# Selective attention and a SwiGLU block on one core: every transpose on TensorE, no DRAM scratch, loads in another order

## The chip, the cores and the metric

The kernel runs on one core of one Trainium2 chip. The metric is device time in microseconds (us) of one launch, the median of several runs. A profiled execution has a time of its own, and inside it the span that the trace covers.

## What is computed

Inputs are q, k and v of 8 batches x 8 heads x 576 positions x 64, a gate s of 8 x 8 x 576, and the three matrices of a gated feed-forward block (FFN): 512 x 1536 twice, and 1536 x 512. All are float32; the output is 4608 x 512 float32.

```python
scores = scale * q @ k^T                       # per batch and head, causal
cum  = cumsum(maximum(s, 0))                   # along the positions
bias = -(cum[i] - cum[j])
attn = softmax(where(causal, -1e9, scores + minimum(bias, 0)))
x    = (attn @ v), heads side by side          # 4608 x 512
g    = x @ w_gate
out  = (g * sigmoid(g) * (x @ w_val)) @ w_out
```

## The kernel before

**Attention.** The 64 heads (batch x head) are numbered in one row, `bh`, and grouped in 16 blocks `hb` of four. A block's q and k are loaded as float32 with positions on partitions (`load_qk`, L105), cast to bf16 in pairs of heads (`cast_one`, L170), and have to be turned so that the 64 features lie on partitions. Two heads share one turned tile. The bias goes into the same matmul: the partitions that the pair's other head would take hold rows with the cumulative sum as a high and a low bf16 part, and rows of ones (`aug`, L155, copies such rows for one block; they were written once to a DRAM tensor `augd` at L153). So one matmul per piece gives score plus bias. Each head's causal half is cut into four score pieces of at most 512 columns (`score_piece`, L253). ScalarE takes their exponential into `pt` (L272), GpSimd masks the diagonal blocks (L276 and L281), and fifteen small matmuls multiply by v (`av_piece`, L288), with a column of ones that yields the softmax's sum. VectorE divides (`av_out`, L305). The division's result `ot` has positions on partitions.

**Who turns what.** Blocks 0 and 1 are turned on TensorE (`pe_transpose`, L200: six transposes of 96 x 128 per pair of heads and tensor into one PSUM tile `tps`, which two copies take out, one per half). From block 2 on the cast block is written to DRAM (`scratch`, L178), read back by a transposing DMA (`transposes`, L187), and split by four VectorE copies (`split`, L192). The FFN needs `xt`, that is x with its features on partitions. Tile 0 is turned on TensorE (`x_pe`, L333). For tiles 1 to 8 GpSimd's queue writes `ot` to a DRAM tensor `xdr` (`x_write`, L320), and SyncE's queue reads it back with a transposing DMA (`x_load`, L329).

**The FFN** (`ffn_items`, L412) works on nine tiles of 512 rows. Each has twelve gate blocks `pg` and twelve value blocks `pv` of four 512-column matmuls, with a tanh on ScalarE and two VectorE operations that empty the two PSUM tiles (`pp`, `ht`), and then four output blocks `py` of twelve matmuls. After each four matmuls the generator yields: 36 items per tile.

**Order.** The order is written out by hand (`manual_schedule`); every engine works through its own list in that order. `attn_items` (L385) yields the attention's pieces with a position, and `pump` (L478) advances it. Up to position 9.2 (heads 0 to 8, called the start below) the attention runs nearly alone. Then each FFN item is followed by as much attention as brings it forward by eight heads per tile, so heads run through tiles 0 to 6, and tiles 7 and 8 have none. `side` (L345) hangs the preparation of the next block on the four heads of this one. A list `wq` of weight loads with their casts is taken from during the start and tile 0; each cast stands in VectorE's list directly behind its load.

**Queues and buffers.** SyncE's queue (SP) issues nearly all loads, the bias rows, scratch writes, transposing reads and the output. PSUM has three tiles for scores, one for `av`, and four in the pool `mp` that `pg`, `pv`, `py`, `tps` and `xps` share.

Of the kernel before, what the change touches and what calls it, by code (L numbers as in the profile page):

```python
# [12 lines left out]
FP32 = mybir.dt.float32  # L13
# [6 lines left out]
def kernel(  # L20
# [42 lines left out]
    def pt_col(tj, bi):  # L63
# [5 lines left out]
    raw = ctx.enter_context(tc.tile_pool(name="raw", bufs=2))  # L69
# [3 lines left out]
    otp = ctx.enter_context(tc.tile_pool(name="otp", bufs=2))  # L73
    wst = ctx.enter_context(tc.tile_pool(name="wst", bufs=2))
    xtp = ctx.enter_context(tc.tile_pool(name="xtp", bufs=2))
# [5 lines left out]
    dram = ctx.enter_context(  # L81
        tc.tile_pool(name="dram", bufs=1, space=bass.MemoryType.DRAM)
    )
# [9 lines left out]
    KX = [[const.tile([128, NR * S + 64], BF16, name=f"k{e}{i}") for e in range(2)] for i in range(2)]  # L93
    QX = [[const.tile([128, NR * S], BF16, name=f"q{e}{i}") for e in range(2)] for i in range(2)]
    VT = [const.tile([128, NCH, H, D + 1], BF16, name=f"vt{i}") for i in range(2)]
    ident = const.tile([128, 128], BF16)
    s_sb = const.tile([BH, S], FP32)
    one_s = const.tile([BH, S], FP32)
    c8 = const.tile([BH, S], FP32)
    hl = const.tile([BH, 4, S], BF16)  # L100

    with tc.manual_schedule():
        loaded = {}

        def load_qk(hb):  # L105
            b, g = divmod(hb, 2)
            for name, src in (("k", k), ("q", q)):
                t = raw.tile([NP, HB, J, D], FP32, tag="raw" + name, name="raw" + name)
                nc.sync.dma_start(
                    t,  # L110
                    src[b, g * HB : (g + 1) * HB, :, :].rearrange(
                        "h (p j) d -> p h (j d)", j=J
                    ),
                )
                loaded[name, hb] = t

        def load_v(b):
            t = raw.tile([128, 4, H, D], FP32, tag="rawv", bufs=1, name="rawv")
            for c in range(4):
                nc.sync.dma_start(  # L120
                    t[:, c, :, :],
                    v[b, :, c * 128 : (c + 1) * 128, :].rearrange("h p d -> p h d"),
                )
            tl = raw.tile([TAIL, H, D], FP32, tag="rawvt", bufs=1, name="rawvt")
            nc.sync.dma_start(tl, v[b, :, 512:S, :].rearrange("h p d -> p h d"))
            loaded["v", b] = (t, tl)

        nc.scalar.dma_start(s_sb, s.rearrange("b h n -> (b h) n"))
        load_qk(0)
        load_v(0)  # L130
# [5 lines left out]
        def init_x(i, eng):  # L136
            for T in (KX[i], QX[i]):
                eng.memset(T[0][64:128, :], 0.0)  # L138
                eng.memset(T[0][64:68, :], 1.0)
                eng.memset(T[1][0:64, :], 0.0)  # L140
                eng.memset(T[1][0:4, :], 1.0)
            for e in range(2):
                eng.memset(KX[i][e][64 * e : 64 * e + 64, NR * S :], 0.0)

        init_x(0, nc.gpsimd)

        nc.scalar.activation(s_sb, s_sb, AF.Relu, scale=8.0)
        nc.vector.tensor_tensor_scan(c8, one_s, s_sb, 0.0, ALU.mult, ALU.add)
        nc.vector.tensor_copy(hl[:, 0, :], c8)
        nc.vector.tensor_sub(hl[:, 1, :], c8, hl[:, 0, :])  # L150
        nc.scalar.mul(hl[:, 2, :], hl[:, 0, :], -1.0)
        nc.scalar.mul(hl[:, 3, :], hl[:, 1, :], -1.0)
        nc.scalar.dma_start(AUG, hl)  # L153

        def aug(hb, eng):  # L155
            for T, k0 in ((KX, 0), (QX, 2)):
                for e in range(2):
                    r0 = 64 * (1 - e) + k0
                    eng.dma_start(
                        T[hb % 2][e][r0 : r0 + 2, 0 : NR * S].rearrange(  # L160
                            "a (r s) -> a r s", r=NR
                        ),
                        AUG[hb * HB : (hb + 1) * HB, k0 : k0 + 2, :].rearrange(
                            "(r e) a s -> e a r s", e=2
                        )[e],
                    )
# [3 lines left out]
        def cast_one(hb, name, r, eng):  # L170
            if r == 0:
                cts[name, hb] = cp.tile([NP, NR, J, 2, D], BF16, tag="c" + name, bufs=1, name="c" + name)
            eng.tensor_copy(  # L173
                cts[name, hb][:, r].rearrange("p j e d -> p e j d"),
                loaded[name, hb][:, 2 * r : 2 * r + 2, :, :],
            )

        def scratch(hb):  # L178
            for name, SC in (("k", KS), ("q", QS)):
                nc.sync.dma_start(  # L180
                    SC[hb].rearrange("(r p j) c -> p r (j c)", r=NR, j=J),
                    cts[name, hb].rearrange("p r j e d -> p r (j e d)"),
                )

        prs = {}

        def transposes(hb):  # L187
            for name, SC in (("k", KS), ("q", QS)):
# [347 lines left out]
```

## Time and profile before

| | us |
|---|---|
| median of 3 runs | 490.84 |
| range of the runs | 487.07 to 491.25 |
| the profiled execution | 488.75 |
| its span | 486.5 |
| TensorE busy in the span | 379.5 |
| VectorE, ScalarE, GpSimd busy | 241.8, 200.6, 159.5 |

The profile names instructions by line, engine, operation and tiles (`out<-in`). Busy time of TensorE counts overlapping matmuls as one stretch, and the end of a matmul is modelled. PEclk is the clock that TensorE was granted. A row of the timeline has its start, its length, engine, line, operation and count, and in brackets how long the engine had stood idle before it and what ended that. A row of the view by stage has the stretch, its length, then per engine the busy time and the count of instructions, then granted clock, the DMA engines' busy share and GB/s.

### The profile page before, as it was taken

Reading aid. Unit: us, or ns where it says so; the run is one execution under the profiler, and the core shown is the slowest. Engines: PE = TensorE matmul, PEld = TensorE weight load, DVE = VectorE, ACT = ScalarE, POOL = GpSimd, SP = SyncE. Lnnn points to the kernel's source line nnn. Section 1 sums busy time; section 2 is a strip of 40 time slices with the busy share of each in tenths; the row PEclk is TensorE's granted clock in tenths of the full one; section 3 lists DMA queues with packets and bytes.
Section 4 is the critical chain, followed back from the end, with each engine's and each line's share of the span. In section 5 each row is a group of like instructions: output and inputs, shape, how many; then the busy total and the mean of one; then the engine's idle time right before and its main releaser. Section 6 shows DMA issues by size and latency. Waiting matters only on the chain.

```text
span 486.5 us, 7669 instructions
## 1 busy us (share of the span) xinstructions
PE 379.5 (78%) x2844; PEld 205.6 (42%) x2896; DVE 241.8 (50%) x438; ACT 200.6 (41%) x406; POOL 159.5 (33%) x273
## 2 busy tenths in 40 slices
PE   0262325296958996899599959995999999999996
PEld 0251223153534553455345525552555554444442
DVE  3453340466615761576167616751775475273670
ACT  2152123044534553455346524652564663232321
POOL 8973133033531462236124612561255211000000
PEclk9997577588997999799889988998999999999999
DMA  9679887957598559845984698379743600701102
GB/s 177 153 211 202 246 221 154 271 140 223 144 214 195 116 131 233 202 106 140 246 189 97 160 232 198 79 186 229 180 77 110 168 2 5 203 13 45 43 0 88
DMA packets 118773, 73.33 MB, mean 151 GB/s; under 512 B 89424, under 2 KB 111440, under 8 KB 118736
## 3 DMA queue, kind: packets, MB, share of 16 engines
q1 hardware_dynamic: 117288, 68.19, 59.1%
q0 software_dynamic: 1264, 4.20, 2.8%
q8 instruction: 23, 0.38, 0.3%
q10 hardware_dynamic: 184, 0.46, 0.3%
q14 instruction: 14, 0.11, 0.1%
HBM read 38.19 MB, written 22.18 MB: 124 GB/s over the span
## 4 chain that ended last, share of the span: by engine, by line
PE 57%; DMA 16%; POOL 11%; SPq 5%; issue 5%; DVE 2%; ACT 1%; another core or an unknown queue 0%; POOLq 0%; ACTq 0%; DVEq 0%
PE pv L432 18%; PE pg L419 18%; PE py L443 11%; DMA xt<-xdr 7%; PE sc L264 6%; PE av L297 4%; SPq L120 3%; DMA wld<-in_moe_w_out_dram 3%; DMA rawq<-in_q_dram 3%; DMA wld<-in_moe_w_val_dram 2%; POOL cq L173 2%; POOL pt L276 1%; DMA wld<-in_moe_w_gate_dram 1%; DMA xdr<-ot 1%; POOL ck L173 1%
## 5 line engine op out<-in xcount | busy, mean ns | idle before, releaser
L272 ACT ACTIVATE pt<-sc 128x512 bf16<-128x512 f32 (+1 forms) x256 | 118.7, 503 | 88.8 <-PE sc L264 88.3
L419 PE MATMUL pg<-xt,wg 128*128 128x512 bf16 x412 | 115.7, 398 | 43.3 <-DMA xt<-xdr 30.7
L426 DVE SCALAR_TENSOR_TENSOR pp<-th,pg 128x512 bf16<-128x512 bf16 x108 | 74.0, 685 | 98.3 <-ACT th L424 97.4
L432 PE MATMUL pv<-xt,wv 128*128 128x512 bf16 x416 | 113.7, 392 | 4.6 <-DVE ht L437 3.5
L424 ACT ACTIVATE th<-pg 128x512 bf16<-128x512 f32 x108 | 64.5, 597 | 125.3 <-PE pg L419 118.9
L443 PE MATMUL py<-wo,ht 128*128 128x512 bf16 x416 | 103.0, 379 | 0.7
L276 POOL TENSOR_SCALAR_AFFINE_SELECT pt<-pt 128x512 bf16<-128x512 bf16 x64 | 41.6, 649 | 166.5 <-ACT pt L272 166.3
L264 PE MATMUL sc<-q,k 128*128 128x128 bf16 (+4 forms) x576 | 79.2, 255 | 18.2 <-DMA q<-augd 8.6
L437 DVE TENSOR_TENSOR ht<-pp,pv 128x512 bf16<-128x512 bf16 x108 | 74.1, 686 | 10.1 <-PE pv L432 1.2
L264 PEld LDWEIGHTS <-k 128*128 128x128 bf16 x576 | 49.6, 104 | 57.4 <-POOL q L138 8.8
L419 PEld LDWEIGHTS <-wg 128*128 128x128 bf16 x432 | 38.9, 101 | 78.7 <-issue 47.8
L297 PE MATMUL av<-vt,pt 128*128 128x65 bf16 x960 | 51.5, 198 | 22.1 <-DVE ot L313 20.4
L297 PEld LDWEIGHTS <-pt 128*128 128x128 bf16 x960 | 45.9, 101 | 49.7 <-issue 24.3
L432 PEld LDWEIGHTS <-wv 128*128 128x128 bf16 x432 | 38.3, 101 | 40.4 <-issue 8.6
L443 PEld LDWEIGHTS <-ht 128*128 128x128 bf16 x432 | 38.0, 98 | 35.3
L312 DVE RECIPROCAL rc<-av 128x5 f32<-128x5 f32 x64 | 12.2, 190 | 68.6 <-PE av L297 68.5
L451 ACT COPY ysb<-py 128x512 f32<-128x512 f32 x36 | 21.1, 586 | 51.8 <-PE py L443 45.7
L281 POOL TENSOR_SCALAR_AFFINE_SELECT pt<-pt 128x64 bf16<-128x64 bf16 x64 | 17.3, 271 | 69.6 <-ACT pt L272 68.9
L313 DVE TENSOR_TENSOR ot<-av,rc 128x320 bf16<-128x320 f32 x64 | 31.4, 491 | 2.2
L173 POOL CAST cq<-rawq 96x768 bf16<-96x768 f32 x30 | 23.9, 826 | 0.0
L173 POOL CAST ck<-rawk 96x768 bf16<-96x768 f32 x30 | 23.9, 825 | 0.0
L221 POOL CAST vt<-rawv 128x512 bf16<-128x512 f32 x32 | 18.7, 617 | 0.1
(48 smaller groups left out, 115.0 us busy)
## 6 DMA issues: line engine op xcount, KB each, us to landing
rawk<-in_k_dram SPq DMA_DIRECT2D x16, 576.0 KB
rawq<-in_q_dram SPq DMA_DIRECT2D x16, 576.0 KB
out_dram<-ysb SPq DMA_DIRECT2D x36, 256.0 KB
rawv<-in_v_dram SPq DMA_DIRECT2D x32, 256.0 KB
ks<-ck SPq DMA_DIRECT2D x14, 288.0 KB
qs<-cq SPq DMA_DIRECT2D x14, 288.0 KB
xdr<-ot POOLq DMA_DIRECT2D x7, 512.0 KB, 5.4
wld<-in_moe_w_gate_dram SPq DMA_DIRECT2D x4, 768.0 KB
```

The lines of the kernel that those rows point to most:

```text
L173: eng.tensor_copy(cts[name, hb][:, r].rearrange("p j e d -> p e j d"), loaded[name, hb][:, 2 * r : 2 * r + 2, :, :],)
L264: nc.tensor.matmul(sc[:, o : o + w], kt[:, r * S + 128 * tj : r * S + 128 * (tj + 1)], qt[:, r * S + lo : r * S + hi], start=True, stop=True,)
L272: nc.scalar.activation(pt[:, CHUNK_PT[ci] : CHUNK_PT[ci] + o], sc[:, 0:o], AF.Exp, scale=0.125)
L276: nc.gpsimd.affine_select(pt[:, 1088:1600], pt[:, 1088:1600], pattern=[[0, 4], [1, 128]], compare_op=ALU.is_ge, fill=zreg, base=0, channel ...
L297: nc.tensor.matmul(av[:, bi * (D + 1) : (bi + 1) * (D + 1)], pt[:, c0 : c0 + 128], VT[b % 2][:, tj, h, :], start=(tj == 0), stop=(tj == bi),)
L313: nc.vector.tensor_mul(ot[:, :, h * D : (h + 1) * D], av3[:, :, 0:D], rc[:, :, None].to_broadcast([128, NCH, D]),)
L419: nc.tensor.matmul(pg, WG[j][:, c, f0 : f0 + 128], xt[:, c, :], start=(c == 0), stop=(c == 3),)
L424: nc.scalar.activation(th, pg, AF.Tanh, scale=0.5)
L426: nc.vector.scalar_tensor_tensor(pp, in0=th, scalar=1.0, in1=pg, op0=ALU.add, op1=ALU.mult)
L432: nc.tensor.matmul(pv, WV[j][:, c, f0 : f0 + 128], xt[:, c, :], start=(c == 0), stop=(c == 3),)
L437: nc.vector.tensor_mul(ht, pp, pv)
L443: nc.tensor.matmul(py, hts[ft][:, ts_ * 128 : (ts_ + 1) * 128], WO[ft // 3][:, ft % 3, :], start=(ft == 0), stop=(ft == NFT - 1),)
```

## The change

- The four DRAM tensors are gone, and with them `scratch`, `transposes`, `split`, `x_write` and `x_load`.
- All 16 blocks of q and k go through `pe_transpose`. From block 2 on VectorE copies the first half of each `tps` and ScalarE the second.
- `ot` is a tile of two heads. `x_pe` turns each pair's five chunks on TensorE into a PSUM tile `xps`; two VectorE copies take it to the two FFN tiles that a batch of 576 rows falls into.
- k and q of one parity share a tile `kq`. The bias rows are copied from SBUF (`HL`) by one DMA per head and side: eight per block in place of four. The minus sign sits in rows of -1. Block 0's are issued by ScalarE and GpSimd, block 1's by GpSimd, the others by SP.
- The start ends after head 7; heads 8 to 63 follow during tiles 0 to 6. Weight loads and casts are parted, three staging buffers in place of two, with the casts at written places (`hook`, and `side` of block 1). Several pools have three buffers in place of two.
- Block 2's and block 3's casts and transposes stand in one piece ahead of their first head, inside FFN tile 0.

```diff
-    KS = [dram.tile([NR * S, 128], BF16, name=f"ks{i}") for i in range(NHB)]
-    QS = [dram.tile([NR * S, 128], BF16, name=f"qs{i}") for i in range(NHB)]
-    AUG = dram.tile([BH, 4, S], BF16, name="augd")
-    xdr = dram.tile([NT, DM], BF16, name="xdr")
...
+        def aug(hb, *engs):
+            for hh in range(HB):
+                eng = engs[hh * len(engs) // HB]
+                r, e = divmod(hh, 2)
+                r0 = 64 * (1 - e)
+                for kq in range(2):
+                    a0 = r0 + 2 - 2 * kq
                     eng.dma_start(
...
+                        KQ[hb % 2][e][a0 : a0 + 2, kq, r * S : (r + 1) * S],
+                        HL[hb * HB + hh : hb * HB + hh + 1, :, :],
                     )
...
+        def x_pe(pr):
+            b, r = divmod(pr, H // 2)
+            ot = ots.pop(pr)
...
+            ps = mp.tile([128, S], BF16, tag="m", name="xps")
+            for c in range(NCH):
+                n = 128 if c < 4 else TAIL
                 nc.tensor.transpose(
...
+                    ps[:, c * 128 : c * 128 + n], ot[0:n, c, :], ident[0:n, 0:n]
+                )
+            n0 = TT - 64 * b
+            nc.vector.tensor_copy(xts[b + 1][:, r, 0 : S - n0], ps[:, n0:S])
+            nc.vector.tensor_copy(xts[b][:, r, TT - n0 : TT], ps[:, 0:n0])
...
+            if NPE <= h + 1 < NHB:
+                if step == 0:
+                    aug(h + 1, nc.sync)
+                    for nm in ("k", "q"):
+                        cast_one(h + 1, nm, 0, nc.gpsimd)
                 if step == 1:
                     for nm in ("k", "q"):
...
+                        cast_one(h + 1, nm, 1, nc.gpsimd)
+                    pe_transpose(h + 1, "k", 0, (nc.vector, nc.scalar))
                 if step == 2:
+                    pe_transpose(h + 1, "q", 0, (nc.vector, nc.scalar))
+                    pe_transpose(h + 1, "k", 1, (nc.vector, nc.scalar))
+                if step == 3:
+                    pe_transpose(h + 1, "q", 1, (nc.vector, nc.scalar))
...
+        LAG = 1.65
+        start = H + 1.45
+        pump(start)
+        hook = {
+            1: [lambda: w_cast("v", 1), lambda: w_load("g", 3)],
+            2: [lambda: load_v(1, range(5))],
+            9: [lambda: w_cast("g", 2), lambda: w_load("v", 3)],
+            10: [lambda: w_cast("v", 2), lambda: w_load("o", 0)],
+            11: [lambda: load_qk(3)],
+            15: [lambda: w_cast("g", 3), lambda: w_load("o", 1)],
+            16: [lambda: w_cast("v", 3), lambda: w_load("o", 2)],
+            19: [lambda: w_cast("o", 0), lambda: w_load("o", 3)],
+            20: [lambda: w_cast("o", 1)],
+            21: [lambda: load_qk(4)],
+            22: [lambda: w_cast("o", 2)],
+            23: [lambda: w_cast("o", 3)],
+        }
...
+            span = 36
+            n0 = 7 if tt == 0 else 0
...
+                pump(lo + (hi - lo) * min(1.0, max(0, n - n0) / (span - n0)))
```

On SP's queue at the end of FFN tile 0, before (`ks`, `qs` are the q and k scratch, `xt` is tile 1's input):

```order
L180 DMA ks_101<-ck 96x2x768
L180 DMA qs_117<-cq 96x2x768
L120 DMA rawv<-in_v_dram 128x8x64 x4
L125 DMA rawvt<-in_v_dram 64x8x64
L452 DMA out_dram<-ysb 128x512
L331 DMA_TRANSPOSE xt<-xdr 128x4x512
```

Scratch writes and transposing reads stand between the loads and the output. With the change the same queue in FFN tile 0 reads, from the first piece of w_out (`wld`) over block 3's q and k to block 3's bias rows (`kq_108`):

```order
L206 DMA wld<-in_moe_w_out_dram 128x3x512
L101 DMA rawk<-in_k_dram 96x4x384
L101 DMA rawq<-in_q_dram 96x4x384
L206 DMA wld<-in_moe_w_out_dram 128x3x512
L119 DMA rawv<-in_v_dram 128x8x64 x2
L206 DMA wld<-in_moe_w_out_dram 128x3x512
L119 DMA rawv<-in_v_dram 128x8x64 x2
L119 DMA rawv<-in_v_dram 64x8x64
L206 DMA wld<-in_moe_w_out_dram 128x3x512
L158 DMA kq_108<-HL 2x1x576 x2
```

No transposing read is left, and a block's small bias copies stand behind all loads that were written ahead of them.

GpSimd's list at the first head, before and with the change (`pt` is a head's exponentials, the two masks being 512 and 64 wide):

```order
L472 MEMSET vt_151 64x8x64
L276 AFFINE_SELECT pt<-pt 128x512
L281 AFFINE_SELECT pt<-pt 128x64
L276 AFFINE_SELECT pt<-pt 128x512
L173 CAST ck<-rawk 96x2x6x64 x2
L173 CAST cq<-rawq 96x2x6x64 x2
```

```order
L462 MEMSET vt_111 64x8x64
L244 AFFINE_SELECT pt<-pt 128x512
L158 DMA kq_108<-HL 2x1x576 x2
L158 DMA kq_109<-HL 2x1x576 x2
L158 DMA kq_108<-HL 2x1x576 x2
L158 DMA kq_109<-HL 2x1x576 x2
L249 AFFINE_SELECT pt<-pt 128x64
```

Block 1's eight bias copies now stand between head 0's two masks, and the casts of block 1 have left this list for VectorE's.

ScalarE's list in the middle of a tile, with the change (`tps` is a PSUM tile of turned q or k, `th` the FFN's tanh):

```order
L240 ACTIVATE pt<-sc 128x512 [waits PE_49,Pool_49]
L416 ACTIVATE th<-pg 128x512 [waits PE_49,Activation_49]
L240 ACTIVATE pt<-sc 128x512 [waits PE_49]
L187 COPY kq_109<-tps 64x576 [waits DVE_49]
L240 ACTIVATE pt<-sc 128x512 [waits PE_49]
L240 ACTIVATE pt<-sc 128x64 [waits PE_49]
```

ScalarE's copy of its half of a `tps` is new there; it waits for VectorE, which copies the other half, and exponentials stand behind it.

More of the change, by code (lines that the diff above doesn't have):

```diff
@@ L176, in cast_one @@
             )
[L178 to L188, printed above, removed]
[L189 to L198 removed]
         def pe_transpose(hb, name, r, engs):
[L201 removed]
+            kq = SRC[name][1]
             ps = mp.tile([128, J, NP], BF16, tag="m", name="tps")
@@ L352, in side, with attn_items @@
+        def attn_items():
+            for kk in range(BH + 4):
+                first = kk < H + 2
+                bh = kk if first else kk - 2
+                b_lo, b_hi = (0, H) if first else (H, BH)
+                h, step = divmod(bh, HB)
+                if not first and step == 0 and 2 <= h < NPE:
+                    aug(h, nc.sync)
                     for nm in ("k", "q"):
-                        pe_transpose(1, nm, 0, (nc.vector, nc.vector))
-                if step == 3:
+                        cast_one(h, nm, 0, nc.gpsimd)
@@ L388, in attn_items @@
+                if bh < b_hi:
                     for ci in range(4):
```

363 lines of the change are left out of this document (161 added, 202 removed).

## The prediction

> **What bounds the kernel now.** I read the page's engine and slice rows first, then the view by stage, then who TensorE waited for.
>
> ```profile
> span 486.5 us, 7669 instructions
> PE 379.5 (78%) x2844; PEld 205.6 (42%) x2896; DVE 241.8 (50%) x438; ACT 200.6 (41%) x406; POOL 159.5 (33%) x273
> PEclk9997577588997999799889988998999999999999
> DMA  9679887957598559845984698379743600701102
> ```
>
> TensorE is the only engine near its limit, and its granted clock dips at even distances. The stages, cut at the first `pg` of each tile, say where the missing 107 us are:
>
> ```profile
> 23.20:75.40 52.20, 22.05 (x249) 17.17 (x251) 20.59 (x38) 16.40 (x38) 22.67 (x42) 0.75 0.83 209
> 75.40:147.60 72.20, 47.49 (x372) 25.89 (x379) 31.35 (x58) 26.07 (x56) 21.79 (x38) 0.83 0.79 197
> 147.60:196.30 48.70, 42.12 (x330) 22.77 (x336) 25.16 (x48) 23.37 (x48) 17.53 (x31) 0.92 0.72 166
> 292.20:339.30 47.10, 41.22 (x330) 22.54 (x336) 24.97 (x48) 23.37 (x48) 17.74 (x31) 0.93 0.75 172
> 339.30:382.10 42.80, 41.88 (x331) 22.66 (x337) 25.08 (x48) 23.05 (x48) 16.89 (x30) 0.96 0.58 135
> 480.20:486.50 6.30, 2.13 (x10) 0.88 (x9) 0.00 (x0) 0.96 (x2) 0.00 (x0) 0.98 0.22 83
> ```
>
> Nothing is dense before 147.6. Tiles 1 to 4 take 191.7 us (147.6 to 339.3), 47.9 each; tile 5, whose successor's input is there almost in time, takes 42.8. The waits name the rest:
>
> ```profile
> PE pg L419 <- DMA xt<-xdr: 30.7, 6, 6.9
> PE av L297 <- DVE ot L313: 20.4, 5, 14.5
> PE pg L419 <- DVE pp L426: 11.3, 1, 11.3
> PE sc L264 <- DMA q<-augd: 8.6, 1, 8.6
> PE sc L264 <- DVE q L195: 8.3, 1, 8.3
> ```
>
> The first row is the DRAM round trip of the attention output, at the turn of a tile. The second and third are VectorE standing in front of a weight cast whose load has not landed:
>
> ```profile
> 52.90 0.96 DVE L229 CAST wg<-wld 128x1536 bf16<-128x1536 f32 x1 [12.34 <-DMA wld<-in_moe_w_gate_dram]
> 88.25 0.96 DVE L229 CAST wg<-wld 128x1536 bf16<-128x1536 f32 x1 [13.87 <-DMA wld<-in_moe_w_gate_dram]
> 117.49 0.96 DVE L231 TENSOR_SCALAR wo<-wld 128x1536 bf16<-128x1536 f32 x1 [0.18 <-DMA wld<-in_moe_w_out_dram]
> ```
>
> So until 117.5 the kernel is bound by loads, and after that by TensorE with a hole per tile.
>
> **A dense stage.** Four 512-column matmuls take 0.867 us (from the first of these rows to the second), so a tile's 36 items take 31.2.
>
> ```profile
> 420.21 1.04 PE L419 MATMUL pg<-xt,wg 128*128 128x512 bf16 x4
> 421.08 1.03 PE L432 MATMUL pv<-xt,wv 128*128 128x512 bf16 x4
> 196.34 1.87 PE L419 MATMUL pg<-xt,wg 128*128 128x512 bf16 x4 [6.26 <-DMA xt<-xdr]
> 382.08 1.02 PE L419 MATMUL pg<-xt,wg 128*128 128x512 bf16 x3 [0.61 <-DMA xt<-xdr]
> ```
>
> After a hole of 6 us the same four matmuls take 1.87: the clock has dropped, and about two items run at half speed, 1.9 us in all. Tile 5 began that way and ended with a wait of 0.6, so eight heads cost 42.8 - 31.2 - 1.9 - 0.6 = 9.1 us, 1.14 each, and a dense stage 40.3. Removing the round trip is thus worth 7.6 us for each of tiles 1 to 4; the same hole stands before tile 1.
>
> **What is added on TensorE.** 14 blocks x 24 = 336 transposes of q and k, and 160 - 16 = 144 of x (32 of them 64 wide).
>
> ```profile
> 33.73 0.67 PE L205 MATMUL tps<-ident,ck 96*128 96x96 bf16 x6
> 34.20 0.68 PE L205 MATMUL tps<-ident,cq 96*128 96x96 bf16 x6
> 61.45 0.38 PE L338 MATMUL xps<-ident,ot 128*128 128x128 bf16 x4
> 73.31 0.60 PE L338 MATMUL xps<-ident,ot 128*128 128x128 bf16 x4 [0.81 <-DVE ot L313]
> L205 PE MATMUL tps<-ident,cq 96*128 96x96 bf16 x24 | 2.7, 279 | 1.0 <-POOL cq L173 0.8 <-DVE cq L173 0.3
> L338 PE MATMUL xps<-ident,ot 128*128 128x128 bf16 x16 | 2.0, 263 | 0.8 <-DVE ot L313 0.8
> ```
>
> Six q/k transposes start 0.47 us apart, 0.078 each, in a stretch where TensorE had just idled. The x transposes appear at both speeds: four in 0.60 after a wait, four in 0.38 in a running stream. Their spacing, with the last one's 0.22 to 0.28 of run-through taken off, is 0.04 to 0.055 warm. From below 336 x 0.041 + 144 x 0.045 = 20 us, from above 336 x 0.078 + 144 x 0.10 = 41. Inside the dense stages the warm row is the nearer: 0.045 and 0.055, that is 48 x 0.045 + 20 x 0.055 = 3.3 us per stage. The stage becomes 43.6.
>
> The Trainium skill, "TensorE: Matmul & The Clock Gate", Part 4 on transposes, speaks against the change: about 275 ns for a 128 x 128 transpose inside a kernel, and the clock's fast state not engaging for them. Its figure is near the mean duration of one (263 and 279 ns), but the trace's spacing is a quarter of that or less; taken as spacing it gives the slower rival below.
>
> **What is added on the other engines.**
>
> ```profile
> L216 DVE COPY q<-tps 64x576 bf16<-64x576 bf16 x7 | 5.3, 753 | 0.1
> L214 ACT COPY k<-tps 64x576 bf16<-64x576 bf16 x1 | 0.6, 635 | 7.8 <-DMA q<-augd 7.8
> L343 DVE COPY xt<-xps 128x512 bf16<-128x512 bf16 x4 | 1.7, 416 | 0.7 <-PE xps L338 0.7
> L195 DVE COPY k<-pk 64x1152 bf16<-64x1152 bf16 x28 | 15.9, 569 | 0.4
> ```
>
> Per stage VectorE gets 8 x 0.753 + 4 x about 0.55 (two copies for 576 columns) = 8.2 us and loses four copies of k and four of q, about 4: 25.0 becomes some 29.3 of 43.6. ScalarE gets 8 x 0.635: 23.4 becomes 28.5. Both fit, and the matmuls hide them. What counts is order: ScalarE's copy waits for VectorE's, so a `tps` holds one of four `mp` buffers for at least 0.753 + 0.635 = 1.39 us. If no other buffer were free, eight per stage would cost 11.1 us; with three others, 2.6 us of matmuls cover it and the cost is 0. VectorE has a third of its time free, so I take 1.2 per stage, nearer the lower end: **44.8**.
>
> SP's queue loses 28 scratch writes, 28 transposing reads and 8 `xt` reads and gains four small copies per block. They are needed a block later, some 20 us, and cost nothing unless loads ahead of them are late, as in tile 0.
>
> **The start** sets the rest. GpSimd's initial work is about as long as before, so its first mask stays near 27 us; then eight bias copies stand ahead of the second.
>
> ```profile
> 27.31 0.64 POOL L276 TENSOR_SCALAR_AFFINE_SELECT pt<-pt 128x512 bf16<-128x512 bf16 x1
> 28.00 1.01 PE L297 MATMUL av<-vt,pt 128*128 128x65 bf16 x15 [1.48 <-POOL pt L276]
> 40.28 0.62 PE L297 MATMUL av<-vt,pt 128*128 128x65 bf16 x15 [1.75 <-DVE ot L313]
> L322 POOL DMA_DIRECT2D xdr<-ot x8 | 4.4, 551 | 15.6 <-DVE ot L313 15.6
> L324 POOL DMA_DIRECT2D xdr<-ot x7 | 5.6, 795 | 0.0
> 0.00:23.20 23.20, 2.28 (x24) 1.88 (x25) 10.09 (x14) 4.50 (x6) 21.52 (x29) 1.00 0.87 173
> 43.00:60.00 17.00, 3.43 (x46) 2.98 (x46) 3.53 (x7) 1.49 (x4) 2.08 (x5) 0.51 0.91 240
> 82.00:98.00 16.00, 3.63 (x17) 1.66 (x18) 6.54 (x10) 0.60 (x1) 0.00 (x0) 0.55 0.97 262
> ```
>
> Eight copies at 0.551 to 0.795 are 4.4 to 6.4 us, so the first `av` comes at 33 rather than 28, although the first score no longer waits 8.6 us for the rows from DRAM. Heads 0 to 3 then cost 4.1 each (28.00 to 40.28 for three), as VectorE evacuates block 1 among them; heads 4 to 7 some 2.6. Head 5, where the first weight cast frees a staging buffer, is reached at about 48, and FFN tile 0 begins near 56, against 75.4.
>
> But loads bind. By the shapes, everything ahead of block 3's bias copies is 19.0 MB: five q/k blocks (1.18 each; block 5's stands ahead of block 3's), three batches of v (1.18), twelve weight pieces (0.79), s 0.15. At 173 GB/s 4.0 MB are in by 23.2; at 240 the next 3.2 by 36.5. Then the queue waits for the staging buffer until 48. The other 11.8 MB at 240 to 262, say 250, take 47 us, and a small copy some 2 more: 97. Head 12's scores, item 20 of tile 0, cannot start before. Before, the trace stands at 118 there with 2.6 heads more done.
>
> **The sum.** 97, then tile 0's 16 remaining items 13.9, 5.6 heads 6.4, their transposes 1.9, clock 1.5; six stages x 44.8 = 268.8; two tiles without attention 62.4; 3.9 after the last matmul (6.3 less the ten matmuls of 480.2). That is 455.8 of span against 486.5. The profiled execution was 488.75, 2.25 more than its span, and the runs' median 0.4% above it: 458.
>
> **Rivals.**
>
> *Evacuation binds.* ScalarE, queued behind VectorE, delays tanh, and TensorE runs out of `mp` buffers. For it: the serial pair of copies. Against it: tiles 7 and 8 run without a hole at 33 of 60 us of VectorE. At 40% of the upper price, 4.5 a stage instead of 1.2, 20 us more: 478.
>
> *The start is not shortened.* The loads keep the pace of the two start stages, 197 to 209 GB/s, so 11.8 MB take 58 us instead of 47; and each of GpSimd's eight copies stands behind a VectorE operation of 0.753, which makes them 1.55 each and everything behind head 5 some 7 us later. Together 18: 476. For it: those stages were loads and little else, too. Against it: their rates hold transposing reads, which are gone. The Trainium skill, "SBUF — State Buffer", on the bandwidth-pool intuition, has a copy from GpSimd's queue grow from 620 to 3100 ns beside a VectorE copy; by that the eight are 25 us and the time 478, and no row here shows it.
>
> *Loads are faster.* Without transposing reads beside them they run at the 262 GB/s of the last row above throughout, and the gap before head 5 is filled: from 23.2 on 15.0 MB take 57 us, a copy 2, so item 20 is at 82: 443. Against it: the staging buffers, three for twelve weight pieces.
>
> *Slower: transposes stand alone.* Each waits for the one before, at its duration: 336 x 0.279 + 144 x 0.263 = 132 us in place of 23, 458 + 109 = 567. It decides from a spacing of (32 + 23)/480 = 0.115 us on. For it: the mean durations. Against it: all four rows of spacing.
>
> **How the numbers follow.** Forecast 0.58; evacuation 0.16; start 0.10; faster loads 0.09; transposes alone 0.05; 0.02 for none of these. The range reaches from 437, below the faster loads, to 484, above evacuation and start with some of both. About 1% is what a measurement of this kernel tells from no change. Slower by more takes the fourth rival, 0.05; within 1% (486 to 496) takes evacuation and start together, 0.04; faster 0.91.
>
> **What would show it.** No TensorE wait for `xt` at the turn of a tile, and stages of tiles 1 to 6 of 44 to 46 us at a clock near 1.00; x transposes in groups of 0.3 us; FFN tile 0 beginning near 56 and a wait of TensorE for `kq` before head 12 ending near 97. The forecast is wrong if stages exceed 47 with waits for `tps` copies, or if a load, not TensorE, ends the waits after tile 0.

## The result, and the profile after

The changed kernel takes 455.73 us, the median of four runs (455.19 to 457.12), against 489.35 of the kernel before in the same series: a ratio of 0.9319, 95% interval 0.9266 to 0.9373, or 33.6 us less. The forecast was 458, its range 437 to 484. The profiled execution took 455.19, its span is 453.5. In two of the series below one execution was disturbed and is left out of median and range; for "more loads moved" that was the profiled one, so its trace is not read.

The page's engine and slice rows of the changed kernel:

```profile
span 453.5 us, 8650 instructions
PE 398.2 (88%) x3319; PEld 225.8 (50%) x3376; DVE 266.2 (59%) x501; ACT 232.7 (51%) x461; POOL 148.1 (33%) x262
PEclk9999888859999999999999999999999999999999
DMA  9970679977690069006900790173011001101002
```

TensorE does 18.7 us more in 33 us less. The clock's dips at even distances are gone after the start, and the DMA engines rest between the tiles' loads. Of the 33.0 us less of span 25.1 lie ahead of tile 1, which begins at 122.52 instead of 147.63, and 7.7 in the six stages behind it (264.84 instead of 272.58). The view by stage, cut at the start of tile 0, at head 12's scores and at the turns of tiles (stretch, length, busy time and count on TensorE, weight loads, VectorE, ScalarE, GpSimd, then clock, DMA share, GB/s):

```profile
26.60:50.20 23.60, 15.14 (x219) 12.08 (x221) 15.67 (x35) 10.29 (x24) 14.57 (x27) 0.99 0.44 119
50.20:96.50 46.30, 30.25 (x215) 15.99 (x218) 28.20 (x45) 18.50 (x35) 10.45 (x18) 0.79 0.86 217
96.50:122.50 26.00, 24.68 (x240) 15.18 (x246) 12.32 (x26) 15.84 (x32) 13.85 (x24) 0.91 0.68 159
166.80:211.30 44.50, 44.00 (x403) 25.62 (x407) 27.75 (x58) 27.92 (x57) 15.92 (x29) 1.00 0.46 105
387.40:449.70 62.30, 62.02 (x284) 28.05 (x287) 33.01 (x48) 19.01 (x32) 0.00 (x0) 1.00 0.09 34
```

A stage has 44.0 of 44.5 us of TensorE at a clock of 1.00. Of TensorE's waits from 123 to 387 one row is left, where the kernel before had 30.7 us for `xt` in the whole execution:

```profile
PE av L265 <- DVE ot L281: 0.9, 1, 0.9
```

What is still loose lies ahead of 96.5: GpSimd's eight bias copies between two masks, the first weight cast, the load that had waited for it, and head 12's scores, which wait for block 3's bias rows.

```profile
26.49 4.08 POOL L158 DMA_DIRECT2D kq<-HL  x8
42.88 0.39 SPq L206 DMA_DIRECT2D wld<-in_moe_w_val_dram  x1
96.49 1.54 PE L232 MATMUL sc<-kq 128*128 128x128 bf16 x9 [5.79 <-DMA kq<-HL]
```

The groups of transposes in a dense stretch, and the odd ones by shape:

```profile
107.73 0.42 PE L178 MATMUL tps<-ident,cq 96*128 96x96 bf16 x6
107.98 0.42 PE L178 MATMUL tps<-ident,ck 96*128 96x96 bf16 x6
121.54 0.52 PE L297 MATMUL xps<-ident,ot 128*128 128x128 bf16 x5
121.99 0.48 PE L265 MATMUL av<-vt,pt 128*128 128x65 bf16 x10
L297 PE MATMUL xps<-ident,ot 64*128 64x64 bf16 x32 | 6.4, 200 | 0.0
```

Six q/k transposes occupy TensorE for 0.25 us, from one group's start to the next (107.73 to 107.98): 0.042 each. Five x transposes take 0.45, from 121.54 to 121.99, though they have the same 576 columns; the fifth is a 64 x 64 one.

### The profile page after: what moved, and what is told of

Its sections match the earlier page's. It is cut to its first block, busy times and chain, and to the rows that moved or that the text cites. A ratio compares the mean times of both kernels' runs of the same rounds, so it can differ in the third digit from the quotient of the medians.

```text
span 453.5 us, 8650 instructions
## 1 busy us (share of the span) xinstructions
PE 398.2 (88%) x3319; PEld 225.8 (50%) x3376; DVE 266.2 (59%) x501; ACT 232.7 (51%) x461; POOL 148.1 (33%) x262
## 4 chain that ended last, share of the span: by engine, by line
PE 68%; DVE 10%; ACT 5%; POOL 5%; DMA 5%; SPq 3%; issue 2%; ACTq 0%; POOLq 0%
PE py L435 20%; PE pg L411 16%; PE pv L424 15%; PE sc L232 7%; PE av L265 6%; DVE pp L418 3%; DVE kq L189 3%; DMA wld<-in_moe_w_out_dram 2%; PE tps L178 2%; PE xps L297 2%; ACT th L416 2%; ACT kq L187 2%; SPq L158 2%; POOL kq L158 2%; DMA rawq<-in_q_dram 2%
## 5 line engine op out<-in xcount | busy, mean ns | idle before, releaser
L424 PE MATMUL pv<-xt,wv 128*128 128x512 bf16 x411 | 111.1, 386 | 1.8 <-DMA kq<-HL 0.2
L411 PE MATMUL pg<-xt,wg 128*128 128x512 bf16 x412 | 110.6, 384 | 1.4 <-issue 0.5
L232 PE MATMUL sc<-kq 128*128 128x128 bf16 (+4 forms) x576 | 79.4, 250 | 14.7 <-DMA kq<-HL 9.6
L232 PEld LDWEIGHTS <-kq 128*128 128x128 bf16 x576 | 47.4, 102 | 47.0 <-issue 6.3
L187 ACT COPY kq<-tps 64x576 bf16<-64x576 bf16 x60 | 38.0, 633 | 48.6 <-DVE kq L189 47.8
L424 PEld LDWEIGHTS <-wv 128*128 128x128 bf16 x432 | 39.6, 99 | 37.9 <-issue 4.9
L265 PEld LDWEIGHTS <-pt 128*128 128x128 bf16 x960 | 41.6, 99 | 33.7 <-POOL pt L244 7.3
L189 DVE COPY kq<-tps 64x576 bf16<-64x576 bf16 x68 | 49.4, 745 | 11.9 <-PE tps L178 11.7
L249 POOL TENSOR_SCALAR_AFFINE_SELECT pt<-pt 128x64 bf16<-128x64 bf16 x64 | 15.8, 246 | 109.4 <-ACT pt L240 109.3
L193 POOL CAST vt<-rawv 128x512 bf16<-128x512 f32 (+1 forms) x40 | 24.2, 629 | 12.4 <-DMA rawv<-in_v_dram 12.4
```

The lines of the kernel that those rows point to most:

```text
L187: nc.scalar.copy(dst, srcp)
L189: engs[e].tensor_copy(dst, srcp)
L232: nc.tensor.matmul(sc[:, o : o + w], T[:, 0, r * S + 128 * tj : r * S + 128 * (tj + 1)], T[:, 1, r * S + lo : r * S + hi], start=True, sto ...
L265: nc.tensor.matmul(av[:, bi * (D + 1) : (bi + 1) * (D + 1)], pt[:, c0 : c0 + 128], VT[b % 2][:, tj, h, :], start=(tj == 0), stop=(tj == bi),)
L411: nc.tensor.matmul(pg, WG[j][:, c, f0 : f0 + 128], xt[:, c, :], start=(c == 0), stop=(c == 3),)
L424: nc.tensor.matmul(pv, WV[j][:, c, f0 : f0 + 128], xt[:, c, :], start=(c == 0), stop=(c == 3),)
```

## The experiments

Three questions: what did each half of the change bring, what do the additions cost, and what binds the start. Ahead of each result stands what was expected before the run: a theory, its rivals, and the time that each gives. Where two intervals of the ratio overlap, the medians alone do not part the kernels. The table has all runs; "stage" is the mean of the five stages from the first `pg` of tile 1 to that of tile 6 in the profiled execution, "tile 1" the first of these.

| kernel | median (runs) | ratio to before, 95% | tile 1 | stage |
|---|---|---|---|---|
| before | 489.35 | | 147.63 | 46.89 |
| the change | 455.73 (455.19 to 457.12) | 0.9266 to 0.9373 | 122.52 | 44.43 |
| x through DRAM | 463.94 (463.33 to 466.40) | 0.9477 to 0.9545 | 137.17 | 42.81 |
| x through DRAM, v loads ahead | 473.45 (472.20 to 474.80) | 0.9604 to 0.9699 | 141.60 | 43.94 |
| q/k through DRAM | 452.08 (451.17 to 452.81) | 0.9232 to 0.9283 | 127.90 | 42.86 |
| q/k transposes twice | 466.36 (465.61 to 467.32) | 0.9517 to 0.9580 | 124.97 | 46.19 |
| evacuations twice | 519.08 (518.32 to 519.94) | 1.0582 to 1.0682 | 140.28 | 52.68 |
| fifth x transpose full | 452.65 (449.98 to 454.54) | 0.9221 to 0.9305 | 120.20 | 43.97 |
| early loads | 447.84 (447.02 to 451.53) | 0.9142 to 0.9231 | 118.62 | 44.47 |
| more loads moved | 446.65 (444.65 to 446.98) | 0.9089 to 0.9179 | | |
| more moved, fifth full | 442.41 (440.28 to 444.63) | 0.9026 to 0.9116 | 110.70 | 43.92 |
| bias copies on ScalarE | 451.47 (450.45 to 452.95) | 0.9210 to 0.9278 | 119.49 | 44.43 |
| mixed | 436.05 (435.30 to 436.58) | 0.8891 to 0.8963 | 113.63 | 42.57 |
| mixed, copies on ScalarE | 431.13 (429.81 to 431.43) | 0.8785 to 0.8855 | 108.22 | 42.86 |

### Which half took the holes away

**x back through DRAM, q/k on TensorE.** The `ot` tiles, DRAM tensor and lag of the kernel before come back for tiles 1 to 8:

```diff
-        LAG = 1.65
+        LAG = 2.9
...
+            nc.sync.dma_start_transpose(xts[tt], xdr[tt * TT : (tt + 1) * TT, :])
...
+            nc.gpsimd.dma_start(xdr[b * S + 512 : (b + 1) * S, :], ot[0:TAIL, 4, :])
...
-            21: [lambda: load_qk(4)],
+            18: [lambda: load_qk(4)],
```

> The changed kernel, with x of tiles 1 to 8 again written to DRAM and read back by a transposing DMA, one batch behind; q and k stay on TensorE. Theory (the round trip is a hole of about 5.7 us plus 1.9 of slow clock at each of the turns to tiles 1 to 5, and the x transposes on TensorE cost 1.8 us per tile): 5 x 7.6 less 7 x 1.8, some 25 us more, about 481 us, TensorE waiting for xt 25 to 31 us. Rival (the hole came from the q and k transposing reads in the same queue, and an xt read alone is nearly free): 450 to 460 us.

Measured: 463.94, between the two. My theory, that the round trip of x makes the holes, fails for the dense stages. The waits of the whole execution, and the starts of two tiles with no wait before them:

```profile
PE pg L429 <- DMA xt<-xdr: 7.2, 2, 4.2
223.80 1.03 PE L429 MATMUL pg<-xt,wg 128*128 128x512 bf16 x4
266.28 1.03 PE L429 MATMUL pg<-xt,wg 128*128 128x512 bf16 x4
```

Two waits are left, before tile 1 and before tile 7; stages between them take 42.48, two us less than with x on TensorE. The trip itself shows why. In this kernel, and then in the kernel before (same lag), the write, the transposing read and, there, the matmul that waited for it:

```profile
256.43 0.53 POOL L294 DMA_DIRECT2D xdr<-ot  x1 [2.05 <-DVE ot L285]
260.38 1.91 SPq L303 DMA_TRANSPOSE xt<-xdr  x1
```

```profile
228.22 0.53 POOL L322 DMA_DIRECT2D xdr<-ot  x1 [1.24 <-DVE ot L313]
232.13 4.32 SPq L120 DMA_DIRECT2D rawv<-in_v_dram  x4
238.23 3.28 SPq L331 DMA_TRANSPOSE xt<-xdr  x1
243.96 1.86 PE L419 MATMUL pg<-xt,wg 128*128 128x512 bf16 x4 [5.64 <-DMA xt<-xdr]
```

Before, the read was issued 10.0 us after the write, behind q/k scratch and v loads on SP's queue, took 3.28 to issue, and tile 3, which waited for it, started 15.7 us after the write. Here it is issued 4.0 us after the write, takes 1.91, and tile 4 starts unhindered 9.85 us after the write. The difference is 5.9, about the hole of 5.64. But two things have changed on the queue: the q/k trips are gone, and the v loads stand behind the read. The next kernel puts the v loads ahead again.

What this one loses lies elsewhere: tile 1 starts 14.65 us later than in the change (head 12's scores, at 102.77, are 6.3 late, and 3.0 are the wait for `xt`), and tile 7 begins with a wait of 4.16. The lateness of head 12 goes with the edit's own order of loads. The edit moved block 4's q and k from item 21 of tile 0 to item 18, and on SP's queue they now stand ahead of block 3's bias copies, for which TensorE waits 13.6 us there:

```profile
91.80 0.61 SPq L105 DMA_DIRECT2D rawk<-in_k_dram  x1
92.46 0.48 SPq L105 DMA_DIRECT2D rawq<-in_q_dram  x1
93.57 9.38 SPq L162 DMA_DIRECT2D kq<-HL  x8
```

In the change the copies are issued at 91.91 and those loads behind them, at 97.67. So the 463.94 prices x through DRAM together with this move and with the longer lag; the stages are the part that can be compared.

**The same with the v loads ahead of the read**, from batch 3 on:

```diff
                 if h % 2 == 0:
-                    if step == 2:
+                    d = 1 if h == 2 else -1
+                    if step == 1 + d:
                         load_v(bn, (0, 1))
-                    if step == 3:
+                    if step == 2 + d:
                         load_v(bn, (2, 3, 4))
```

> The kernel with x through DRAM again, with one thing altered: from batch 3 on the v loads of the next batch stand on SyncE's queue just ahead of the transposing read of x, as they did in the kernel before, instead of behind it; q and k stay on TensorE. One theory says that x's round trip was long before because of the q/k scratch writes and transposing reads beside it: then stages stay at 42.4 to 42.9 with hardly a wait for xt, and the time at 462 to 466 us. The other says that the v loads ahead of it on the queue (4.3 us of issue in the row before) made it long: then TensorE waits 3 to 6 us for xt at the turn of tiles 3 to 6, stages of 46 to 48 there, 478 to 490 us.

Measured: 473.45, between the two, but the turns of the tiles speak for the first theory. The write, the v loads, the read and the matmul at tile 3, and the waits at tiles 1 and 4:

```profile
221.22 0.53 POOL L294 DMA_DIRECT2D xdr<-ot  x1 [2.05 <-DVE ot L285]
221.07 2.27 SPq L123 DMA_DIRECT2D rawv<-in_v_dram  x3
227.00 2.94 SPq L303 DMA_TRANSPOSE xt<-xdr  x1
232.23 1.02 PE L430 MATMUL pg<-xt,wg 128*128 128x512 bf16 x4 [1.00 <-DMA xt<-xdr]
```

```profile
275.72 1.02 PE L430 MATMUL pg<-xt,wg 128*128 128x512 bf16 x4 [0.84 <-DMA xt<-xdr]
141.60 1.86 PE L430 MATMUL pg<-xt,wg 128*128 128x512 bf16 x4 [8.32 <-DMA xt<-xdr]
```

With the v loads ahead the trip takes 11.0 us and the wait is 0.5 to 1.6 at tiles 2 to 5, not 5.3 to 6.3 as before. So v loads in this place cost about 1 us, and the q/k trips, with what they push back, make up the other 4.7 (15.7 less 11.0). The two are not fully parted: here the v loads are issued together with the write, and what the read then waits for on SP's queue is the write's landing (2.2 us ahead of 227.00). In the kernel before, the v loads stood behind the q/k scratch writes and were issued from 232.13 on, up to just ahead of the read, which had no write left to wait for. At tile 1, where the loads of the start are still running, the wait is 8.3 us instead of 3.0. In the profiled executions, 11.4 us apart in span, tile 1 starts 4.4 us later and the six stages are 5.7 longer.

**q/k of blocks 4 to 15 back through DRAM, x on TensorE.**

```diff
-                    pe_transpose(h + 1, "k", 0, (nc.vector, nc.scalar))
+                    scratch(h + 1)
...
-                    pe_transpose(h + 1, "q", 0, (nc.vector, nc.scalar))
-                    pe_transpose(h + 1, "k", 1, (nc.vector, nc.scalar))
+                    transposes(h + 1)
...
-                    pe_transpose(h + 1, "q", 1, (nc.vector, nc.scalar))
+                    split(h + 1, "k", nc.vector)
+                    split(h + 1, "q", nc.vector)
```

> The changed kernel, with q and k of blocks 4 to 15 again written to DRAM, read back by transposing DMAs and split by VectorE; x stays on TensorE. Theory (the transposes cost TensorE 0.042 us each and the DRAM way is hidden behind a block of work): 12 x 24 x 0.042 = 12 us less, about 444 us, stages of 42.3. Rival (the DRAM way costs waits for VectorE's split or crowds the queue): 456 to 475 us.

Measured: 452.08, again between the two: 3.6 us faster than the full change in the medians and in the profiled spans (449.9 against 453.5), though the ratios' intervals overlap. The stages are 42.86 against 44.43, where the theory had 42.3; tile 1 starts 5.4 us later, which takes three fifths of it back (the six stages give 9.0). That is the rival at work: between head 12 and tile 1 TensorE waits 4.4 us for VectorE's split of the first block that comes through DRAM, which the change does not have. Either half alone therefore rids the stages of their holes, and doing both costs TensorE time in the stages that it did not have to spend there.

### What the additions cost

**Every q/k transpose issued twice** (the second writes the same again, the output is unchanged):

```diff
-            for j in range(J):
+            for j in list(range(J)) * 2:
```

> The changed kernel with every q and k transpose issued twice into the same place. Theory (spacing 0.042 us, TensorE is the bound in the stages): 384 x 0.042 = 16 us more, about 472 us, stages of 46.5. Rival 1 (TensorE waits for evacuation anyway, so the second pass is hidden): 455 to 460. Rival 2 (a transpose costs its duration of 0.22 to 0.28 us): 540 us or more.

Measured: 466.36, 10.6 more: two thirds of what the theory gave, and far from the rival of transposes in series. A stage grows by 1.76 us for 48 more transposes, 0.037 each; at that rate the 336 of the change cost 12.4. Two stages of its trace are 171.16 to 217.35 and on, with no wait of TensorE but the 0.9 us already there:

```profile
171.16 1.03 PE L411 MATMUL pg<-xt,wg 128*128 128x512 bf16 x4
217.35 1.03 PE L411 MATMUL pg<-xt,wg 128*128 128x512 bf16 x4
```

**Every evacuation of q/k made twice**, the transposes once:

```diff
-            for e in range(2):
+            for e in (0, 1) * 2:
                 dst = KQ
```

> Every copy of q/k out of the transposes' PSUM tile is made twice (VectorE, ScalarE, VectorE, ScalarE), the transposes once: per stage 6.0 us more of VectorE (8 of 0.745) and 5.1 us more of ScalarE (8 of 0.633), and the chain of one group lengthens from 1.4 to 2.8 us. The theory, that evacuation lies beside TensorE's work because a stage has 27.5 us of VectorE and 28.6 of ScalarE in 44.4, gives at most 2 us more per stage: 455 to 468 us. The rival, that evacuation holds up the next transposes or the scores of the block, gives 8 times 1.4 or 11 us more per stage for six stages: 515 to 525 us.

Measured: 519.08, slower than the kernel before. The rival is right: 8.25 us more per stage. Who TensorE waited for from 140 to 404, the five stages:

```profile
PE pv L424 <- ACT kq L187: 17.9, 15, 1.6
PE pg L411 <- ACT kq L187: 7.7, 10, 0.9
PE py L435 <- ACT kq L187: 4.3, 5, 0.9
```

The FFN's matmuls wait for the copy that gives a `tps` buffer back to the pool `mp` that they share, 6.0 us a stage (VectorE's `pp` and `ht` make another 0.7). Eight chains of 1.38 us were added (0.745 and 0.633), 11.0 in all, of which 2.8 were hidden: 0.34 us a group. So in the change the evacuation costs TensorE no wait, but its cover, the time for which a group may hold its buffer before TensorE waits, is by this estimate about 1.7 us, the chain's own 1.38 and little more, although VectorE and ScalarE both have a third of their time free. My theory, which argued from that free time, fails. No run changed the number of `mp` buffers, so that they are the limit is read from the waits alone.

**The fifth x transpose made full size** (128 columns from 128 rows; the last 64 are not read):

```diff
-            ps = mp.tile([128, S], BF16, tag="m", name="xps")
+            ps = mp.tile([128, 640], BF16, tag="m", name="xps")
...
-                    ps[:, c * 128 : c * 128 + n], ot[0:n, c, :], ident[0:n, 0:n]
+                    ps[:, c * 128 : c * 128 + 128], ot[:, c, :], ident
```

> The fifth transpose of each pair of heads' x is made 128 columns from 128 rows instead of 64 from 64 (its last 64 columns are not read). The theory, from the group of five that takes 0.45 us where 576 columns at the rate of the q/k transposes are 0.25, is that the odd-shaped transpose costs about 0.2 us by its change of shape: the group shrinks to 0.25 to 0.30 us, a stage from 44.4 to 43.7, and the time is 450 to 452 us. The rival says that the 0.45 us comes with the group as such (its change from one kind of matmul to another and back): no change or a little more, 455 to 457 us.

Measured: 452.65, 3.1 less than the change's median; the two ratios' intervals overlap, so the trace has to carry it. A group there, and the wait that came with it:

```profile
174.73 0.44 PE L296 MATMUL xps<-ident,ot 128*128 128x128 bf16 x5
175.01 0.46 PE L265 MATMUL av<-vt,pt 128*128 128x65 bf16 x10
PE pv L423 <- ACT kq L187: 1.9, 6, 0.3
```

The group takes 0.28 instead of 0.45. Four per stage are 0.68; TensorE now waits 0.3 us a stage for an evacuation, which leaves 0.4, and the stage is 0.46 shorter. The theory is right on the transpose; its 43.7 a stage and 450 to 452 us are missed by little, and that little met the narrow cover just measured.

### What binds the start

**Early loads**: batch 1's v and block 3's q and k right behind block 2's.

```diff
                     load_qk(2)
+                    load_v(1, range(5))
+                    load_qk(3)
...
-            2: [lambda: load_v(1, range(5))],
-            11: [lambda: load_qk(3)],
```

> The changed kernel with the loads of batch 1's v and block 3's q and k issued right behind block 2's, where the DMA engines stand still from 34 to 43 us. Theory (loads alone set when head 12 starts): the gap of 9 us is filled, head 12's scores start near 87 instead of 96.5, about 446 us. Rival (the order of weight casts and bias copies in tile 0 sets it, not the amount loaded): 453 to 457 us.

Measured: 447.84, 7.9 less. The order of the loads binds the start, as the theory has it, though in the profiled execution head 12 starts at 92.77 and not near 87. What is left of the wait ahead of head 12 (the profiled execution was the slowest of the four, 451.53):

```profile
92.77 0.48 PE L232 MATMUL sc<-kq 128*128 128x128 bf16 x3 [5.02 <-DMA kq<-HL]
```

**More loads moved**: block 3's bias copies at item 8 of tile 0 (the `hook` list counts items) instead of with head 12, twelve items later, the output weights ahead of block 5's q and k and of batch 2's v.

```diff
-                    aug(h, nc.sync)
+                    if h == 2:
+                        aug(h, nc.sync)
...
+            8: [lambda: aug(3, nc.sync)],
...
+            21: [lambda: w_cast("o", 1), lambda: load_v(2, range(5))],
...
+            24: [lambda: load_qk(5)],
```

> The loads of the start again, one step further: block 3's q/k and batch 1's v loaded right behind block 2's, and now also the bias copies of block 3 asked for nine hooks earlier on SyncE's queue, and the output weights ahead of block 5's q/k and batch 2's v. The theory says that with q/k and v early the start still waits 5.0 us for block 3's bias copies (row at 92.77 of the run with the early loads), since they stand in SyncE's queue behind loads that wait for a staging buffer: with these gone head 12 starts near 78 to 85 instead of 92.8, tile 1 begins near 105 to 111 instead of 118.6, and the time is 436 to 441 us, stages unchanged at 44.4. The rival says that the weights' own arrival binds there and another wait takes the place: 445 to 448 us.

Measured: 446.65, 1.2 less than early loads, which is within the spread of the runs. The time is the rival's, that another wait takes the place; which one, the next kernel's trace shows.

**The same with the fifth transpose full**, which also gives the trace:

> The earlier loads and bias copies and the full-size fifth x transpose, with all q/k on TensorE: the mixed kernel without its q/k through DRAM. Theory: the start no longer waits for loads but for block 3's own casts and copies, head 12 near 86 to 87 as in the mixed kernel, tile 1 at 113 to 114, stages of 44.0 as with the full-size transpose alone: 444 to 446 us, so that q/k through DRAM were worth 8 to 10 us in the mixed kernel (5 of its stages by 1.8 to 2.0). Rival: TensorE still waits for a DMA ahead of head 12, and the time is that of the early loads less 2.5, 444 to 446 too, but with a row of a wait for bias copies of over 3 us in the trace.

Measured: 442.41, a little under both. Tile 1 (110.70) comes earlier than the theory had it. Head 12 starts at 83.69, and what it waits for is VectorE:

```profile
83.69 1.44 PE L232 MATMUL sc<-kq 128*128 128x128 bf16 x8 [2.46 <-DVE kq L189]
82.90 2.07 DVE L189 COPY kq<-tps 64x576 bf16<-64x576 bf16 x3
```

No DMA is waited for there. Block 3's four groups stand in one piece ahead of head 12, and the wait that took the place is their evacuation, the same chain as above, and not the weights' arrival that the rival of the run before had named.

**Block 1's bias copies on ScalarE** instead of GpSimd, in the changed kernel:

```diff
-                    aug(1, nc.gpsimd)
+                    aug(1, nc.scalar)
```

> The eight bias copies of block 1 are asked for by ScalarE instead of GpSimd, everything else as in the changed kernel. There GpSimd issues them for 4.08 us from 26.49, its next diagonal mask comes at 30.57 and TensorE's second group of av waits for it, while ScalarE has 11.3 us with nothing to do. The theory, that the eight copies delay the heads 1 to 5, hence the first weight cast (41.9), hence the loads that wait for its staging buffer, gives all that follows 3 to 4.5 us earlier: first weight cast near 38, head 12 near 92 to 93, 451 to 453 us. The rival, that the loads set the start by their bytes alone whatever the heads do, gives head 12 at 96 to 97 as before: 455 to 457 us.

Measured: 451.47, as the theory said, 4.3 less than the change (the ratios' intervals overlap a little, the traces part them). The first weight cast starts at 38.18 instead of 41.91, and the load that it lets through is issued 3.7 us earlier:

```profile
38.18 0.95 DVE L214 CAST wg<-wld 128x1536 bf16<-128x1536 f32 x1
39.16 0.39 SPq L206 DMA_DIRECT2D wld<-in_moe_w_val_dram  x1
94.25 1.54 PE L232 MATMUL sc<-kq 128*128 128x128 bf16 x9 [6.98 <-DMA kq<-HL]
```

Of the 3.7 us, 2.2 arrive at head 12, which the theory had at 92 to 93, and 3.0 at tile 1 (119.49) and at the end of the span (450.5 against 453.5).

### A version that beats both

**Mixed**: the moved loads, the full fifth transpose, x on TensorE, q/k on TensorE up to block 5 and through DRAM from block 6 on.

```diff
+                    if h + 1 < 6:
+                        pe_transpose(h + 1, "k", 0, (nc.vector, nc.scalar))
+                    else:
+                        scratch(h + 1)
```

> The earlier loads and bias copies of the start, the fifth x transpose at full size, and the q/k of blocks 6 to 15 through DRAM with transposing DMAs as before the change, while x stays on TensorE. The theory is that the terms add: q/k on TensorE cost a stage 1.8 to 1.9 us (44.4 against 42.1 to 42.7 in the run with q/k through DRAM), the odd x transpose 0.7, the start gives 15 to 19 against the change: stages of 41.7 to 42.2 from tile 2 on, 420 to 428 us. The rival is that the DMA transposes and scratch writes fall into the stretch of the moved loads, or that the early start moves a wait into the next tile: 432 to 445 us.

Measured: 436.05, in the rival's range. Its stages (42.57) miss the 42.2 by little, with one of 44.10 in which TensorE waits for a split; the start gives 8.9 us, from 122.52 to 113.63, where I had 15 to 19. The wait ahead of head 12 and the one for the split:

```profile
86.88 1.44 PE L259 MATMUL sc<-kq 128*128 128x128 bf16 x8 [2.46 <-DVE kq L194]
295.50 0.40 PE L259 MATMUL sc<-kq 128*128 128x128 bf16 x4 [1.59 <-DVE kq L213]
```

The evacuation ahead of head 12 is a wait of 2.46 us, less than the 6 to 10 that the start falls short. With all q/k on TensorE the same wait stands there, and still head 12 starts 3.2 us earlier, at 83.69, and tile 1 at 110.70. From 48.8 to 83.0 us the granted clock was 0.85 here and 0.93 there; why, no run shows. All in all q/k through DRAM gain 6.4 us in the medians (442.41 to 436.05), where 8 to 10 were expected.

**Mixed, with block 1's copies on ScalarE**:

> The mixed kernel with block 1's bias copies asked for by ScalarE instead of GpSimd. Theory: here no load is waited for ahead of head 12, so the 4 us that GpSimd's issues take come off the start in full: 431.5 to 433.5 us. Rival: head 12 now waits for something that the heads do not move (the weight loads, or block 3's q/k): 435 to 437 us.

Measured: 431.13, 4.9 less than mixed and a little better than the theory. It is the fastest kernel of the study, at a ratio of 0.8820 (0.8785 to 0.8855) to the kernel before and 24.6 us under the change.

## Why the prediction was right, point by point

- **A dense stage of 40.3 without transposes** held. From 44.43, the q/k transposes are worth 1.76 (doubled) or 1.57 (taken out) and x on TensorE 1.99 (44.47 for tiles 2 to 5 with it, 42.48 with x through DRAM). That leaves 40.7.
- **The hole of 7.6 per tile** went, as forecast. The cause as the prediction put it, "the DRAM round trip of the attention output", is half of it: it made them while q and k made such trips too, ahead of it on the same queue; without those it made none at tiles 2 to 6, or 0.5 to 1.6 us at tiles 2 to 5 with the v loads put back ahead of it. With x off DRAM and q and k on it there was none either. A forecast for x alone or q/k alone from this step would have been wrong.
- **q/k transposes at 0.045**: 0.042 by spacing, 0.037 by doubling. The "warm" row was the right one to take. The Trainium skill, "TensorE: Matmul & The Clock Gate", Part 4, gives about 275 ns for one and a clock that does not engage. The mean duration here agrees in size (215 and 217 ns), but the spacing, 42 ns, is about a sixth of that figure; the granted clock is 1.00 in stages that hold 68 transposes, but 512-column matmuls run between them, so these stages do not test that rule. The spacing rules out the rival at 567.
- **x transposes at 0.055** is the mis-sized term: 1.1 us per stage forecast, 4 x 0.45 = 1.8 by the rows, 1.99 by the experiment. The 64 x 64 transpose was priced by its columns; it costs 0.17 us more than a full one.
- **Evacuation at 1.2 a stage** measured 0, the lower bound; these two errors nearly cancel, and 44.8 stood against 44.43. But "with three others, 2.6 us of matmuls cover it" was too wide: the cover is some 1.7. So the rival at 478 was closer than its 0.16 said: by that estimate it begins at 0.34 us more per group.
- **The start, 97 at head 12's scores**, measured 96.49, with errors that cancel, which is luck. The forecast had the first weight cast at 48 and tile 0 at 56, and then 250 GB/s; it was 41.9 and 50.2, and then 217 GB/s (the row from 50.20 on). That rate is nearer to the 197 to 209 of the rival in which the start is not shortened; the earlier heads made up for it. GpSimd's eight copies took 4.08 us, 0.51 each, under the lower bound of 4.4. VectorE ran nothing in those 4.08 us, so that rival's wait behind a VectorE operation was not put to the test. The Trainium skill, "SBUF — State Buffer", on the bandwidth-pool intuition, gives a growth to 3100 ns for a copy from GpSimd's queue beside a VectorE copy. These eight do not show it, since no VectorE copy ran beside them. That the copies lie on the path, over the weight cast and the staging buffer, is shown by moving them.
- **From head 12 to tile 1** 26.0 us against 23.7 (13.9 + 6.4 + 1.9 + 1.5); this stretch has a clock of 0.91 and was not broken down further.
- **The sum**: 96.5 + 26.0 + 264.8 (122.52 to 387.36) + 62.3 + 3.8 = 453.5 before rounding, against 97 + 23.7 + 268.8 + 62.4 + 3.9 = 455.8. The six stages were 4.0 too long and the stretch before them 2.3 too short. Two small slips stand in the forecast: its 3.9 is 4.2 by its own row (6.30 less 2.13), and the 458 leaves out the 0.4% that its sentence names.
- **Faster loads, 443**: not by themselves, but with the loads moved head 12 starts at 83.7, near the 82 of that rival, and the time is 442.4 (with the fifth transpose full, alone worth about 3). That comes from the order, with the pause after 34 us filled (188 GB/s from 34 to 43, where the change has 0), not from a higher rate: from 48.8 to 83.0 the loads run at 171 GB/s.
- **Left open**: three quarters of the gain, the 25.1 us ahead of tile 1, is what the prediction got by adding up loads. The two waits behind weight casts that it lists (14.5 and 11.3) are gone. The runs show what binds the start of the changed kernel; none parts the new order of loads, the third staging buffer and the missing DRAM trips against the kernel before.

## What to carry to other kernels

When two kinds of traffic share a queue and one of them is seen to be late, take out either one on paper before paying for both: here moving q and k, or x, off DRAM was each enough for the dense stages, and keeping q and k of the later blocks on DMA was 6.4 us better (442.4 to 436.0) once the start was mended. What hid an evacuation here was how soon its PSUM buffer came back to the pool, not the idle time of the engines that copy; double it once and see. And a start that waits for loads is read backwards: from the last wait to the staging buffer, to the cast that frees it, to whatever stands ahead of that cast.

## What the runs showed of the hardware

A 64 x 64 transpose among 128 x 128 ones made its group of five take 0.45 us instead of 0.28 with a full-size one in its place. The transposing reads of x for tiles 2 to 5 took 3.1 to 3.4 us to issue in the kernel before, 1.9 to 2.9 with v loads ahead of them and q/k on TensorE, and 1.4 to 2.1 with the v loads behind them. Why the odd shape costs more and why the issue of a read varies was not measured.
